# Local attention scores: 36 small products on eight array tiles for 18 products with padded queries

## The chip, the cores and the metric

The kernel runs on one core of a Trainium2 chip. The metric is the device time of one execution in microseconds (us), as the median of several runs. TensorE multiplies (PE in the profile; PEld is its weight loads), VectorE (DVE), ScalarE (ACT) and GpSimd (POOL) do the elementwise work, SyncE (SP) issues transfers. A product's *weights* are the operand that is loaded into the array, its *moving* operand streams through it. The array can be used in parts: a *tile* is a range of its rows and columns, given by the partitions that the operands and the result lie on.

## The reference

Attention over 8 batches and 8 heads with 576 positions of 64 channels, followed by a mixture of 8 experts that sends each token to one expert. The first four heads are local: a query sees the 32 positions that end at its own. The other four see every 32nd position.

```python
scores = scale * np.matmul(q, k.transpose(0, 1, 3, 2))
rel = pos[:, None] - pos[None, :]
mask_local = (rel >= 0) & (rel < stride)
mask_strided = (rel >= 0) & (pos[None, :] % stride == pos[:, None] % stride)
masks = np.stack([mask_local if h < H // 2 else mask_strided for h in range(H)], axis=0)
scores = np.where(masks[None, :, :, :], scores, -1000000000.0)
...
attn = attn / (np.sum(attn, axis=-1, keepdims=True) + 1e-09)
return np.matmul(attn, v).astype(np.float32)
...
for e in range(E):
    mask = e_idx == e
    h = np.maximum(x[mask] @ w1[e], 0.0)
    out[mask] = gate_w[mask, None] * (h @ w2[e])
```

## The kernel before

The attention is cut into 32 units that alternate: a local one (class `Local`, one head of two batches) and a strided one (class `Strided`, two heads of one batch). A unit passes through a pipeline of four steps. In round `n` of the loop over units TensorE does the scores of unit `n`, turns the exponentials of unit `n-2` (`turn`), writes the masks of unit `n+1` into PSUM (`masks`), and multiplies the values of unit `n-3` (`values`). This order on TensorE is written out by hand; the loads on SyncE keep the order of the program; the order on VectorE and ScalarE is set by a scheduler that works from estimated times. A few `warm` products on zeros fill the first rounds. After every four pairs of units a block of routing work (`lg`, `lt`, `en`) is spread over the next rounds. Then come the experts (`ffn`): weights and tokens are gathered, each split in two parts, and multiplied in three products each.

In a local unit a position's queries are cut into 18 blocks of 32. Block `i` of batch `bb` needs two neighbouring key blocks, 64 positions. The tile `qk` has the channels of batch 0 on partitions 0 to 63 and those of batch 1 on 64 to 127; its first 18 blocks are queries, the other 19 keys. So that one product does both batches over all 128 partitions, `prep` copies the queries into `qd`, which is zero elsewhere: batch 0's queries to rows 0 to 63, columns 0 to 31, batch 1's to rows 64 to 127, columns 32 to 63 (VectorE copies one half at L335, ScalarE the other at L333; there are two buffers `qd`, filled with zeros once at L296). The product then has 128 rows, 64 columns of weights and 64 moving columns. Its result lies on 64 partitions, so the 18 products of a unit take turns on two column tiles (`jj`). The nine groups `g` have their scores side by side in PSUM, four in one bank and five in another (`s`), on top of the masks. VectorE takes the maximum (`mx`) and subtracts it (`ex`), ScalarE exponentiates. `turn` transposes, ScalarE copies to `et`, and `values` multiplies with `vv`.

Of the kernel before, what the change touches and what calls it, by code (L numbers as in the profile page):

```python
# [20 lines left out]
P = 128  # L21
# [60 lines left out]
def _place(g, jj):  # L82

    return 16 + jj if g == 8 else 4 * (g // 2) + g % 2 + 2 * jj


def _block(i, bb):

    return (i + 2 * bb) % 18


def _constants():
    cf = np.zeros((P, C_N), np.float32)
    cf[:, C_ID:C_ID + P] = np.eye(P)
    cf[:, C_RE8:C_RE8 + E] = E - np.arange(E)
    cf[:, C_H:C_H + TH] = np.arange(P)[:, None] + P * np.arange(TH)
    cf[:, C_SIO:C_SIO + NBP * LA] = np.arange(NBP * LA)
    cf[:, C_P] = np.arange(P)
    cf[:, C_F:C_F + 4] = P * np.arange(4)
    for i, r0 in enumerate(ROWS):  # L100
        for t in range(4):
            cf[r0 + 18 * t:r0 + 18 * t + 18, C_T + 4 * i + t] = 1
    cb = np.zeros((P, M_N), np.float32)
    cb[:, M_ID:M_ID + P] = np.eye(P)
    qi = np.arange(32)[:, None]
    kk = np.arange(64)[None, :]
    for g in range(9):
        for jj in range(2):
            for bb in range(2):
                ok = (kk > qi) & (kk <= qi + STRIDE)  # L110
                if _block(_place(g, jj), bb) == 0:
                    ok = ok & (kk >= 32)
                r0 = 64 * jj + 32 * bb
                cb[r0:r0 + 32, M_L + 64 * g:M_L + 64 * g + 64] = np.where(ok, 0, BIG)
    a = np.arange(18)
    causal = np.where(a[None, :] <= a[:, None], 0, BIG)
    for j in range(2):
        for h in range(2):
            r0 = 64 * j + 18 * h
            cb[r0:r0 + 18, M_S:M_S + 288] = np.tile(causal, (1, 16))  # L120
    cb[:, M_TRI:M_TRI + P] = -(np.arange(P)[:, None] >= np.arange(P)[None, :]).astype(np.float32)
    cb[:, M_ONE:M_ONE + P] = 1
    tok = P * np.arange(36)[None, :] + np.arange(P)[:, None]
    return cf, cb.astype(ml_dtypes.bfloat16), tok.astype(np.float32)


def _layout(q, k, v, moe_modality_id, moe_w_gate, moe_modality_bias, moe_w1, moe_w2):
# [12 lines left out]
    for bb in range(2):  # L140
        for i in range(18):
            blk = _block(i, bb)
            qkl[:, :, bb, :, i] = qt[:, :, bb, :, blk]
            qkl[:, :, bb, :, 19 + i] = kt[:, :, bb, :, blk]
            w = win[:, :, i % 2, :, 2 * (i // 2) + bb] if i < 16 else win[:, :, i - 16, :, 16 + bb]
            w[:, :, 32:, :D] = vr[:, :, bb, blk]
            if blk:
                qkl[:, :, bb, :, 18 + i] = kt[:, :, bb, :, blk - 1]
                w[:, :, :32, :D] = vr[:, :, bb, blk - 1]
# [17 lines left out]
    mod = mod.reshape(36, P).transpose(1, 0)  # L167
    mb = np.broadcast_to(np.asarray(moe_modality_bias).reshape(1, 2 * E), (P, 2 * E))
    cf, cb, tok = _constants()
    rt = np.concatenate([wg.reshape(P, 128), np.ascontiguousarray(mod).view(np.float32), tok, mb], axis=1)  # L170
    nul = np.zeros((1, 2 + DM), np.int32)
# [20 lines left out]
def attention_moe(ctx: ExitStack, tc: tile.TileContext, a, out):  # L192
    nc = tc.nc
# [6 lines left out]
    def pa(name):  # L200
        return ps.tile([P, 512], F32, tag="a", name=name)
# [35 lines left out]
    pin = tc.keep_in_program_order  # L237
# [31 lines left out]
    def behind_units(ins, of=None):  # L269
        of = spots if of is None else of  # L270
        if of:
            tc.add_manual_dep(ins.ins, of[-1].ins.name, behind, reason="units first")
# [4 lines left out]
    def mark(ins):  # L277
        pace.append(ins)
# [10 lines left out]
    def zeros(n, shape, name):  # L289
        return [lp.tile(shape, F32, bufs=1, name=f"{name}{i}") for i in range(n)]  # L290

    qds = zeros(2, [P, 18, 2, 32], "qd")
    ets = zeros(1, [P, 18, 2, 32], "et")
    qzs = zeros(2, [P, 32, 2, 18], "qz")
    for t in qds + ets:
        nc.vector.memset(t[:], 0.0)  # L296
    for t in qzs:
        nc.gpsimd.memset(t[:], 0.0)
# [6 lines left out]
    class Local:  # L305
# [19 lines left out]
                self.vv.rearrange("p i c -> p (i c)")[:, c], a["vl"][self.bp, self.h, :, c]))  # L325

        def prep(self):
            self.qd = qd = qds[self.n % 2]
            for bb in range(2):
                r = slice(64 * bb, 64 * bb + 64)  # L330
                dst, src = qd[r, :, bb, :], self.qk[r, 0:18, :]
                if bb:
                    pin(nc.scalar.copy(dst, src))  # L333
                else:
                    ins = nc.vector.tensor_copy(dst, src)  # L335
                    pin(ins)
                    behind_units(ins)

        def masks(self):
            self.ss = []  # L340
# [3 lines left out]
                self.ss.append((g0, gn, s.rearrange("p (g c) -> p g c", g=gn)))  # L344

        def scores(self):
            n, qk, qd = self.n, self.qk, self.qd
            mx = lp.tile([P, 9], F32, tag="mx", name=f"mx{n}")
            self.ex = ex = lp.tile([P, 11, 64], F32, tag="ex", name=f"ex{n}")
            for g0, gn, s in self.ss:  # L350
                for g in range(gn):
                    for jj in range(2):
                        i = _place(g0 + g, jj)
                        self.scored = nc.tensor.matmul(  # L354
                            s[64 * jj:64 * jj + 64, g, :],
                            qd[:, i, :, :].rearrange("p b q -> p (b q)"),
                            qk[:, 18 + i:20 + i, :].rearrange("p b q -> p (b q)"),
                            start=False, stop=True, skip_group_check=True,
                        )
                m = mx[:, g0:g0 + gn]  # L360
                ins = nc.vector.tensor_reduce(m, s, AX.X, ALU.max)
                if g0:
                    behind_units(ins)
                nc.vector.tensor_tensor(ex[:, g0:g0 + gn, :], s, m.unsqueeze(2).to_broadcast([P, gn, 64]), ALU.subtract)
                nc.scalar.activation(ex[:, g0:g0 + 4, :], ex[:, g0:g0 + 4, :], AF.Exp, scale=0.125)
            nc.scalar.activation(ex[:, 9:11, :], ex[:, 8:9, :].to_broadcast([P, 2, 64]), AF.Exp, scale=0.125)
# [16 lines left out]
        def values(self):  # L383
            n, et, vv, xt, h = self.n, self.et, self.vv, self.xt, self.h
            for bb in range(2):
                gn = 5 - bb
                o = pa(f"o{n}{bb}")[:, :(D + 1) * gn].rearrange("p (g c) -> p g c", g=gn)
                for k in range(4):
                    for jj in range(2):
                        u = 4 * k + 2 * jj + bb  # L390
                        self.valued = nc.tensor.matmul(  # L391
                            o[64 * jj:64 * jj + 64, k, :], et[:, u, :, :].rearrange("p g q -> p (g q)"), vv[:, u, :],
                            start=True, stop=True, skip_group_check=True,
                        )
                if bb == 0:
                    for b2 in range(2):
                        nc.tensor.matmul(
                            o[64 * b2:64 * b2 + 64, 4, :], et[:, 16 + b2, :, :].rearrange("p g q -> p (g q)"),
                            vv[:, 16 + b2, :], start=True, stop=True, skip_group_check=True,
                        )  # L400
                rs = lp.tile([P, 5], F32, tag="rs", name=f"rs{n}{bb}")
                nc.vector.tensor_scalar(rs[:, :gn], o[:, :, D], 1e-9, None, ALU.add)
                nc.vector.reciprocal(rs[:, :gn], rs[:, :gn])
                mark(nc.vector.tensor_tensor(
                    xt[:, 5 * bb:5 * bb + gn, D * h:D * h + D], o[:, :, 0:D],
                    rs[:, :gn].unsqueeze(2).to_broadcast([P, gn, D]), ALU.mult,
                ))
# [759 lines left out]
    for what in ORDER.split():  # L1167
        i = int(what[1])
# [15 lines left out]
    for n in range(nu + 3):  # L1184
# [13 lines left out]
        if 1 <= n <= nu:  # L1198
            ins = units[n - 1].load_values(0)
# [8 lines left out]
        if 1 <= n <= nu:  # L1208
            ins = units[n - 1].load_values(1)
# [65 lines left out]
    li, _, inc, wall = tables[len(PHASES) - 1]  # L1275
# [38 lines left out]
```

## Time and profile before

| | us |
|---|---|
| Median of three runs (lowest, highest) | 584.99 (580.6, 586.03) |
| The profiled execution | 581.83 |
| Its span, first to last instruction | 580.0 |
| TensorE busy, modelled | 564.3 |
| VectorE, ScalarE, GpSimd busy | 381.7, 325.0, 197.2 |

Busy times are sums over the span. Matmuls overlap in the array, and their ends are modelled, so TensorE's busy time alone doesn't say how dense its work is; the chain of waits and the counts of records do. In the chain, "issue" is time in which an engine waited for nothing that the profile shows. A product of two float32 operands is two records in the trace, each with a weight load of its own.

### The profile page before, as it was taken

The page shows a single profiled execution, that of the slowest core. Times are in us where ns is not written, and L with a number is a line of the kernel's source. Part 1 is how long each engine was busy: PE and PEld are TensorE (multiplying, and loading weights), DVE is VectorE, ACT ScalarE, POOL GpSimd, SP SyncE. Part 2 cuts the span into 40 slices and gives each one's busy share as a digit, 9 for nine tenths or more (in the row PEclk, how much of TensorE's full clock was granted, in tenths as well). Part 3 has the DMA queues.
Part 4 walks back from the last instruction along what each step waited for, and adds up shares of the span by engine and source line. Part 5 has one row for each costly group of instructions (what it writes and reads, how often), then busy time and mean ns, then how long its engine had stood idle before and what let it go on. Part 6 is the DMA issues. An engine that isn't in the chain of part 4 may idle for free.

```text
span 580.0 us, 13584 instructions
## 1 busy us (share of the span) xinstructions
PE 564.3 (97%) x5383; PEld 495.1 (85%) x5385; DVE 381.7 (66%) x909; ACT 325.0 (56%) x646; POOL 197.2 (34%) x198
## 2 busy tenths in 40 slices
PE   9999999998999999999999999999999999999995
PEld 5878888877788899989999998989898998998884
DVE  7886977967867874676674757666475666655410
ACT  5789898897744544554454544545363555545312
POOL 3011120125464315444344334554434445320102
PEclk9999999999999999999999999999999999999999
DMA  8988898978985308566543266142414156772102
GB/s 299 332 287 298 287 326 292 327 229 296 313 296 196 118 12 308 187 199 223 154 164 74 61 211 216 47 88 73 90 33 99 52 200 174 262 162 72 56 0 76
DMA packets 62699, 104.28 MB, mean 180 GB/s; under 512 B 36451, under 2 KB 36963, under 8 KB 58532
## 3 DMA queue, kind: packets, MB, share of 16 engines
q0 software_dynamic: 15456, 57.47, 28.6%
q1 hardware_dynamic: 45636, 43.29, 25.5%
q10 hardware_dynamic: 1536, 2.58, 1.4%
q8 instruction: 44, 0.72, 0.5%
q14 instruction: 27, 0.22, 0.1%
HBM read 94.09 MB, written 19.18 MB: 195 GB/s over the span
## 4 chain that ended last, share of the span: by engine, by line
PE 82%; issue 10%; ACT 3%; DVE 2%; POOL 1%; POOLq 0%; ACTq 0%
PE h L1022 31%; PE o L1037 30%; PE s L354 3%; PE ss L449 3%; PE o L391 2%; PE ot L499 2%; PE lg L597 2%; PE xl L224 2%; PE t L224 2%; PE xs L224 1%; PE warm L212 1%; PE ts L224 1%; POOL out L1044 1%; ACT xc L507 1%; PE en L695 1%
## 5 line engine op out<-in xcount | busy, mean ns | idle before, releaser
L1059 DVE TENSOR_TENSOR wl<-raw,wh 128x512 fp32r<-128x512 f32 x176 | 115.2, 692 | 66.8 <-ACT wh L1058 56.7
L1058 ACT CAST wh<-raw 128x512 fp32r<-128x512 f32 x176 | 100.5, 619 | 99.4 <-PE o L1037 81.5
L1022 PE MATMUL h<-xh,wl 128*128 128x384 f32 x352 | 118.7, 337 | 0.0
L1022 PE MATMUL h<-xl,wh 128*128 128x384 f32 x352 | 118.2, 336 | 0.0
L1022 PE MATMUL h<-xh,wh 128*128 128x384 f32 x352 | 117.4, 337 | 0.0
L1037 PE MATMUL o<-wl,hh 128*128 128x512 f32 x264 | 104.1, 394 | 0.0
L1037 PE MATMUL o<-wh,hl 128*128 128x512 f32 x264 | 104.0, 395 | 0.0
L1037 PE MATMUL o<-wh,hh 128*128 128x512 f32 x264 | 103.2, 391 | 0.0
L1025 ACT ACTIVATE hh<-h 128x384 fp32r<-128x384 f32 x88 | 43.2, 491 | 82.4 <-PE h L1022 71.0
L1027 DVE SCALAR_TENSOR_TENSOR hl<-h,hh 128x384 fp32r<-128x384 f32 x88 | 48.9, 555 | 56.5 <-ACT hh L1025 55.1
L921 POOL DMA_INDIRECT raw<-in_w,wi x44 | 51.8, 1177 | 61.3 <-ACT hh L1025 50.8
L1022 PEld LDWEIGHTS h<-xh,wh 128*128 128x128 f32 x352 | 66.2, 188 | 4.2 <-PE xs L224 0.4
L1022 PEld LDWEIGHTS h<-xl,wh 128*128 128x128 f32 x352 | 66.1, 188 | 2.9
L1022 PEld LDWEIGHTS h<-xh,wl 128*128 128x128 f32 x352 | 66.0, 188 | 0.4 <-DVE wl L1059 0.4
L889 POOL DMA_INDIRECT fx<-xd,le x33 | 37.2, 1129 | 76.8 <-ACT wh L1058 42.2
L1037 PEld LDWEIGHTS o<-wh,hl 128*128 128x128 f32 x264 | 49.5, 188 | 10.5
L1037 PEld LDWEIGHTS o<-wl,hh 128*128 128x128 f32 x264 | 49.5, 188 | 8.6
L1037 PEld LDWEIGHTS o<-wh,hh 128*128 128x128 f32 x264 | 49.6, 188 | 8.2
L906 POOL DMA_INDIRECT le<-ld,li x33 | 35.5, 1076 | 41.9 <-DVE li L828 17.6
L1044 POOL DMA_INDIRECT out<-y,le x33 | 34.6, 1049 | 41.3 <-ACT y L1043 37.0
L589 POOL DMA_DIRECT2D xd<-xt x18 | 10.0, 558 | 64.9 <-ACT xc L507 28.2
L983 DVE COPY work<-fx 128x1536 uint16<-128x1536 uint16 x16 | 27.2, 1743 | 0.0
(215 smaller groups left out, 872.6 us busy)
## 6 DMA issues: line engine op xcount, KB each, us to landing
vv<-in_vl SPq DMA_DIRECT2D x32, 292.5 KB
qks<-in_qks SPq DMA_DIRECT2D x32, 288.0 KB
qk<-in_qkl SPq DMA_DIRECT2D x16, 304.0 KB
qk<-in_qkl SPq DMA_DIRECT2D x16, 288.0 KB
xd<-xt POOLq DMA_DIRECT2D x18, 256.0 KB
vsp<-in_vs SPq DMA_DIRECT2D x16, 256.0 KB
xd<-xt SPq DMA_DIRECT2D x9, 256.0 KB
xd<-xt ACTq DMA_DIRECT2D x2, 1024.0 KB
```

Source lines behind the costliest of these rows:

```text
L224: return nc.tensor.transpose(dst, src, ident)
L889: ins = in_turn(nc.gpsimd.indirect_dma_start(xt[:, h, :], None, xd[0:xrows, :], IOA(ap=le[:, h, 0:1], axis=0), **bounds))
L906: in_turn(nc.gpsimd.indirect_dma_start(le[:, h, :], None, ld[0:1 + last, :], IOA(ap=li[:, s, h:h + 1], axis=0)))
L921: ins = nc.gpsimd.indirect_dma_start(raws[j].rearrange("p f c -> p (f c)"), None, a["w"], IOA(ap=wi[:, s, j:j + 1], axis=0), bounds_check= ...
L983: pin(nc.vector.tensor_copy(rows[:, :, w, :], halves(xt)[:, :, :, w]))
L1022: nc.tensor.matmul(hp, w[:, a1], x[:, c, 0:size], start=(k == 0), stop=(k == 11))
L1025: steps.append(nc.scalar.activation(hh[:, 0:size], hp, AF.Relu))
L1027: nc.vector.scalar_tensor_tensor(hl[:, 0:size], hp, 0.0, hh[:, 0:size].bitcast(F32), ALU.max, ALU.subtract)
L1037: nc.tensor.matmul(os[h], hx[:, m], w[:, 512:1024], start=(f == 0 and i == 0), stop=(f == 7 and i == 2))
L1044: outs.add(in_turn(nc.gpsimd.indirect_dma_start(out, IOA(ap=le[:, i, 0:1], axis=0), y[:], None, bounds_check=NT - 1, oob_is_err=False), True))
L1058: nc.scalar.copy(wh[:, c], raw[:, c])
L1059: nc.vector.tensor_tensor(wl[:, c], raw[:, c], wh[:, c].bitcast(F32), ALU.subtract)
```

## The change

`prep` is empty, and `qd` with its zeros is gone. `scores` makes one product for each batch, block and group: 64 rows (the batch's partitions), 32 columns of weights (the block's queries, straight from `qk`) and 64 moving columns. There are 36 per unit. The result goes to 32 partitions; `_side` exchanges the two batches' partitions in the groups 4 to 8, so that a group of the first bank and one of the second together use all eight tiles of 64 rows by 32 columns. The groups run in the order 0, 4, 1, 5, 2, 6, 3, 7, 8, the maxima and subtractions stand behind all of them, and the masks and the index into `et` follow the exchange.

```diff
+def _side(g, bb):
+
+    return bb ^ (g >= 4)
...
-                r0 = 64 * jj + 32 * bb
+                r0 = 64 * jj + 32 * _side(g, bb)
...
-    qds = zeros(2, [P, 18, 2, 32], "qd")
...
         def prep(self):
-            self.qd = qd = qds[self.n % 2]
-            for bb in range(2):
-                r = slice(64 * bb, 64 * bb + 64)
-                dst, src = qd[r, :, bb, :], self.qk[r, 0:18, :]
-                if bb:
-                    pin(nc.scalar.copy(dst, src))
-                else:
-                    ins = nc.vector.tensor_copy(dst, src)
-                    pin(ins)
-                    behind_units(ins)
+            pass
...
-            for g0, gn, s in self.ss:
-                for g in range(gn):
-                    for jj in range(2):
-                        i = _place(g0 + g, jj)
+            for g in (0, 4, 1, 5, 2, 6, 3, 7, 8):
+                g0, _, s = self.ss[g >= 4]
+                for jj in range(2):
+                    for bb in range(2):
+                        i, r = _spot(g, jj, bb), slice(64 * bb, 64 * bb + 64)
+                        c0 = 64 * jj + 32 * _side(g, bb)
                         self.scored = nc.tensor.matmul(
-                            s[64 * jj:64 * jj + 64, g, :],
-                            qd[:, i, :, :].rearrange("p b q -> p (b q)"),
-                            qk[:, 18 + i:20 + i, :].rearrange("p b q -> p (b q)"),
+                            s[c0:c0 + 32, g - g0, :], qk[r, i, :], qk[r, 18 + i:20 + i, :].rearrange("p b q -> p (b q)"),
                             start=False, stop=True, skip_group_check=True,
                         )
+            for g0, gn, s in self.ss:
                 m = mx[:, g0:g0 + gn]
                 ins = nc.vector.tensor_reduce(m, s, AX.X, ALU.max)
...
-                            o[64 * jj:64 * jj + 64, k, :], et[:, u, :, :].rearrange("p g q -> p (g q)"), vv[:, u, :],
+                            o[64 * jj:64 * jj + 64, k, :],
+                            et[:, 4 * k + 2 * jj + _side(2 * k, bb), :, :].rearrange("p g q -> p (g q)"), vv[:, u, :],
```

`_spot(g, jj, bb)` returns `_place(g, jj)`.

On TensorE, round 4 (the third local unit) reads as follows before; the numbers behind the names are buffers, `x8` counts products:

```order
L354 MATMUL s_367<-qk_198,qd_101 64x64 x8
L354 MATMUL s_369<-qk_198,qd_101 64x64 x10
L224 MATMUL t_432<-cf_sb,ex_260 128x128 x4
L224 MATMUL t_437<-cf_sb,ex_260 128x128
L442 LDWEIGHTS cb_sb
L442 MATMUL ss_444<-cb_sb 128x288
L499 MATMUL ot_446<-eb_361,vsp_113 64x72 x8
L499 MATMUL ot_456<-eb_361,vsp_113 64x72 x8
```

The same place after:

```order
L356 MATMUL s_393<-qk_208 32x64 x4
L356 MATMUL s_395<-qk_208 32x64 x4
L356 MATMUL s_393<-qk_208 32x64 x4
L356 MATMUL s_395<-qk_208 32x64 x4
L356 MATMUL s_393<-qk_208 32x64 x4
L356 MATMUL s_395<-qk_208 32x64 x4
L356 MATMUL s_393<-qk_208 32x64 x4
L356 MATMUL s_395<-qk_208 32x64 x8
L234 MATMUL t_476<-cf_sb,ex_270 128x128 x4
L234 MATMUL t_481<-cf_sb,ex_270 128x128
L444 LDWEIGHTS cb_sb
L444 MATMUL ss_488<-cb_sb 128x288
```

The 18 products became 36, which go to the two banks by turns; what stands behind them is as it was, ten lines further down in the file.

On VectorE, behind the copy `qz` of a strided unit, before:

```order
L438 COPY qz_105<-qks_729 64x32x18
L361 TENSOR_REDUCE mx_901<-s_858 128x4
L468 RECIPROCAL sms_841<-sms_841 128x16
L364 TENSOR_TENSOR ex_902<-s_858,mx_901 128x256
L470 TENSOR_TENSOR enp_111<-exs_838,sms_841 128x288
L361 TENSOR_REDUCE mx_901<-s_860 128x5
L364 TENSOR_TENSOR ex_902<-s_860,mx_901 128x320
L335 COPY qd_101<-qk_802 64x18x32
L461 TENSOR_REDUCE mxs_1013<-ss_941 128x16
```

The corresponding place after:

```order
L440 COPY qz_103<-qks_787 64x32x18
L470 RECIPROCAL sms_915<-sms_915 128x16
L362 TENSOR_REDUCE mx_975<-s_932 128x4
L472 TENSOR_TENSOR enp_107<-exs_912,sms_915 128x288
L362 TENSOR_REDUCE mx_975<-s_934 128x5
L365 TENSOR_TENSOR ex_976<-s_932,mx_975 128x256
L365 TENSOR_TENSOR ex_976<-s_934,mx_975 128x320
L463 TENSOR_REDUCE mxs_1103<-ss_1033 128x16
```

The copy to `qd` is gone, and the second maximum moved ahead of the first subtraction.

## Rows read from the trace of the kernel before

**Rows 1.** Page, part 1: busy us (share) xinstructions, by engine.

```profile
PE 564.3 (97%) x5383; PEld 495.1 (85%) x5385; DVE 381.7 (66%) x909; ACT 325.0 (56%) x646; POOL 197.2 (34%) x198
```

**Rows 2.** Table by stretches: us, busy by engine, granted clock, DMA share, GB/s.

```profile
6.40:18.50 12.10, 11.99 (x301) 9.70 (x303) 10.24 (x30) 8.55 (x19) 0.00 (x0) 1.00 1.01 360
18.50:34.00 15.50, 14.19 (x397) 12.67 (x395) 13.32 (x41) 13.73 (x31) 2.65 (x6) 1.00 0.86 279
34.00:135.00 101.00, 97.83 (x2324) 83.21 (x2322) 81.95 (x319) 88.36 (x204) 18.13 (x28) 1.00 0.89 295
135.00:580.00 445.00, 435.04 (x2355) 387.56 (x2352) 272.39 (x517) 212.22 (x392) 171.78 (x155) 1.00 0.46 145
```

**Rows 3.** The same table for the local scores (L354) alone: PE, PEld.

```profile
0.00:18.50 18.50, 3.76 (x108) 3.40 (x108) 1.00 0.91 312
18.50:34.00 15.50, 2.66 (x72) 2.40 (x72) 1.00 0.86 279
34.00:135.00 101.00, 14.17 (x396) 12.51 (x396) 1.00 0.89 295
```

**Rows 4.** Chain of waits, 38 to 58 us: start us, us, what, records.

```profile
39.14 1.11 issue
...
48.31 1.20 PE s L354 x36
...
51.47 1.86 PE lg L597 x32
...
53.56 1.23 PE ss L449 x64
```

**Rows 5.** Chain of waits, 17 to 34 us.

```profile
18.60 0.59 ACT et L378
...
21.90 0.67 ACT qd L333
...
29.50 0.67 ACT qd L333
...
33.35 0.34 DVE xt L404
```

**Rows 6.** Groups of instructions by line: count, busy us, mean ns, idle before.

```profile
L333 ACT COPY qd<-qk 64x576 f32<-64x576 f32 x16 | 10.7, 668 | 2.7 <-DMA qk<-in_qkl 2.3
...
L335 DVE COPY qd<-qk 64x576 f32<-64x576 f32 x16 | 7.1, 445 | 0.2 <-DMA qk<-in_qkl 0.2
...
L364 DVE TENSOR_TENSOR ex<-s,mx 128x256 f32<-128x256 f32 x16 | 6.5, 406 | 0.0
...
L296 DVE MEMSET qd<- 128x1152 f32 x2 | 2.0, 1018 | 0.4 <-issue 0.4
```

**Rows 7.** Waits of TensorE's weight loads to 135 us: total us, times, longest.

```profile
PEld o L391 <- ACT xt L514: 0.9, 2, 0.5
```

**Rows 8.** Chain of waits, 0 to 150 us.

```profile
1.19 4.94 PE warm L212 x13
...
62.95 0.67 ACT qd L333
...
97.72 0.67 ACT qd L333
```

**Rows 9.** Chain of waits, 107 to 127 us.

```profile
109.22 1.00 PE en L695 x18
...
114.44 0.88 issue
...
125.52 0.36 issue
```

**Rows 10.** Table by stretches for `lg` (L597) alone, its first 0.03 us.

```profile
51.40:51.43 0.03, 0.03 (x4) 0.03 (x4) 1.00 0.65 230
```

**Rows 11.** TensorE's instruction queue: packets, MB, share; whole span (page), then 0 to 135 us.

```profile
q8 instruction: 44, 0.72, 0.5%
...
q8 instruction: 23, 0.38, 1.1%
```

More of the change, by code (lines that the diff above doesn't have):

```diff
@@ L84, in _place, with _spot @@
     return 16 + jj if g == 8 else 4 * (g // 2) + g % 2 + 2 * jj
+def _spot(g, jj, bb):
+    return _place(g, jj)
+def _side(g, bb):
+    return bb ^ (g >= 4)
 def _block(i, bb):
@@ L110, in _constants @@
                 ok = (kk > qi) & (kk <= qi + STRIDE)
-                if _block(_place(g, jj), bb) == 0:
+                if _block(_spot(g, jj, bb), bb) == 0:
                     ok = ok & (kk >= 32)
-                r0 = 64 * jj + 32 * bb
+                r0 = 64 * jj + 32 * _side(g, bb)
                 cb[r0:r0 + 32, M_L + 64 * g:M_L + 64 * g + 64] = np.where(ok, 0, BIG)
@@ L290, in zeros @@
         return [lp.tile(shape, F32, bufs=1, name=f"{name}{i}") for i in range(n)]
-    qds = zeros(2, [P, 18, 2, 32], "qd")
     ets = zeros(1, [P, 18, 2, 32], "et")
     qzs = zeros(2, [P, 32, 2, 18], "qz")
-    for t in qds + ets:
+    for t in ets:
         nc.vector.memset(t[:], 0.0)
@@ L346, in scores @@
         def scores(self):
-            n, qk, qd = self.n, self.qk, self.qd
+            n, qk = self.n, self.qk
             mx = lp.tile([P, 9], F32, tag="mx", name=f"mx{n}")
             self.ex = ex = lp.tile([P, 11, 64], F32, tag="ex", name=f"ex{n}")
-            for g0, gn, s in self.ss:
-                for g in range(gn):
-                    for jj in range(2):
-                        i = _place(g0 + g, jj)
+            for g in (0, 4, 1, 5, 2, 6, 3, 7, 8):
[4 more added lines that the diff above has]
+                        c0 = 64 * jj + 32 * _side(g, bb)
                         self.scored = nc.tensor.matmul(
-                            s[64 * jj:64 * jj + 64, g, :],
-                            qd[:, i, :, :].rearrange("p b q -> p (b q)"),
-                            qk[:, 18 + i:20 + i, :].rearrange("p b q -> p (b q)"),
+                            s[c0:c0 + 32, g - g0, :], qk[r, i, :], qk[r, 18 + i:20 + i, :].rearrange("p b q -> p (b q)"),
                             start=False, stop=True, skip_group_check=True,
                         )
+            for g0, gn, s in self.ss:
                 m = mx[:, g0:g0 + gn]
@@ L397, in values @@
                         nc.tensor.matmul(
-                            o[64 * b2:64 * b2 + 64, 4, :], et[:, 16 + b2, :, :].rearrange("p g q -> p (g q)"),
+                            o[64 * b2:64 * b2 + 64, 4, :], et[:, 16 + _side(8, b2), :, :].rearrange("p g q -> p (g q)"),
                             vv[:, 16 + b2, :], start=True, stop=True, skip_group_check=True,
```

## The prediction

> **What bounds the kernel now.** I read the page first: TensorE is busy for 97% of the span [rows 1]. The profiled execution took 581.83 us, its span 580.0, so 1.83 lie around it; the median of the three runs shown, 584.99, is 3.16 above that execution. I take differences from the profiled execution and subtract them from the median.
>
> The second view is the table by stretches [rows 2]. The local scores (L354) run only up to 135 us; the remaining 445 us are the experts' products, which the change doesn't touch. The granted clock is 1.00 in each stretch shown, so every price below is one at 2.4 GHz. Of the 16 local units three have their scores before 18.5 us, two up to 34 us and eleven between 34 and 135 us (36 records each) [rows 3]. The stretches have different limits. From 6.4 to 18.5 us the 16 DMA engines are full (share 1.01, 360 GB/s). From 34 to 135 us TensorE is busy for 97.8 of 101 us, VectorE and ScalarE for 82 and 88.
>
> The third view is the chain of waits. From 38 to 58 us it is one product after another on TensorE, with a single gap, and a local unit's scores stand in it with 1.20 us [rows 4]. So here a microsecond less on TensorE is a microsecond less in all, as long as the others keep up. From 18.6 to 33.7 us the same view runs through ScalarE and VectorE instead: the copies to `et`, to `xc`, and twice the copy to `qd` with 0.67 us [rows 5].
>
> **What the change removes.** Per local unit it removes the two copies that build `qd`, 0.67 us on ScalarE and 0.45 on VectorE, 16 of each, and at the start two fills of 1.0 us [rows 6]. In the stretch bound by ScalarE both `qd` copies are on the chain: 2 x 0.67 = **1.3 us** come off; the next that is late there is TensorE, which was busy for 14.19 of 15.5 us. Between 34 and 135 us the copies lie beside TensorE's work and I cost them at nothing. Twice the loads of `o` waited for ScalarE's copy to `xt`, 0.9 us in all [rows 7], and the chain has a `qd` copy ahead of such an `o` at 62.95 and at 97.72 us [rows 8]; so I leave out 0.9 us at most. The fills end before the first scores, behind which TensorE has its 4.94 us of `warm` [rows 8]: nothing.
>
> **What it does to the scores.** Before, a unit is 18 products with 64 columns of weights on two column tiles; after, 36 products with 32 columns of weights and half the rows, on eight tiles, and as many moving columns (64) in each. Each product is two records in the trace (36 and now 72). The price hangs on how many tiles run at once.
> One tile: `en` (L695) puts nine products of 64 moving columns into one place; 18 records take 1.00 us [rows 9], 55.6 ns for a record alone on its tile. Two tiles: the scores now, 18 records on each tile, 18 x 55.6 = 1.00 us, and 0.20 to fill and leave. Four tiles: `lg` (L597), eight records per tile of 256 columns, 8 x 4 x 55.6 = 1.78 us, and the chain shows 1.86 [rows 4]. Its records also start together: four products and four weight loads in the first 0.03 us [rows 10]. So the time was each tile's own records one after another plus 0.08 to 0.20, whatever the other tiles did, with one, two and four tiles. After the change the groups 4 to 8 give the busiest tile five products, ten records: 10 x 55.6 = 0.56, plus 0.18 = **0.74 us**, against 1.20. That saves 0.46 per unit.
> Eight tiles, and tiles that share columns but not rows, are not in this trace, so I bound the cost. Below: 72 records at the spacing in which `lg` starts (four in 0.03 us) are 0.54 us, so the tile's own time with the small lead, 0.64, is the floor. Above: the densest long stream is the strided scores, 64 records in 1.23 us, 19.2 ns each [rows 4]; 72 of these are 1.38 us, 0.18 more than now. I take 0.74, since `ss` also runs on two tiles only and loads 36 columns of weights for 18 moving ones, so that its pace is its tiles' and not the stream's.
> In the stretch that TensorE bounds: 11 x 0.46 = **5.1 us**. In the first 18.5 us three units could give 1.4; the DMA engines are full there, `warm` products stand between the units, and I take **0.5**.
>
> **What it adds.** TensorE's program grows by 16 x 36 x 2 = 1152 instructions. Its instructions come by a queue of their own: 44 packets, 0.72 MB in all, for 10,768 records, a packet of 16 KB per 245 of them [rows 1, 11]; 4.7 packets more. Up to 135 us there were 23 [rows 11], and three halts of TensorE inside a run of products with no waiter named: 1.11, 0.88 and 0.36 us [rows 4, 9]. 2.35/23 = 0.10 us per packet, so **0.5 us** more, if the halts are these packets' and come as often.
> On VectorE the order moves: both maxima now stand ahead of both subtractions, since both score tiles end together. A unit's scores end 0.46 us earlier, and its exponentials are needed two units later, so I cost the move at nothing; without that cover one subtraction, 0.41 us a unit [rows 6], would be late. The moved columns of `et` change an index only.
>
> **A rule against it.** Each pair of row halves writes the same PSUM bank in the same round (groups 0 and 4 have one bank each, with both halves in it). No row shows this, since every product before spans all row groups. The Trainium skill, TensorEngine Tiling (Array Packing), section Restrictions and Gotchas, says that different row tiles cannot access the same PSUM bank simultaneously. By that rule the first rival below would hold; its price is worked out from rows there.
>
> **Rivals.** (1) *The halves take turns*: four tiles at once, as in `lg`, and no more. Then 72/4 = 18 records follow each other per column group, as now: 1.20 us, no gain on TensorE. ScalarE's 1.3 us stay, and the 0.5 of the packets: 584.99 - 1.3 + 0.5 = **584.2**. For it: nothing in the trace runs more than four at once. Against it: with one, two and four tiles each tile kept its own time.
> (2) *The stream can't be fed, slower*: a unit takes 144 instructions in 0.74 us, 195 per us, where it took 72 in 1.20, 60 per us, and `ss` 104 per us. TensorE halts for 0.9 to 1.1 us when the next packet is late, as at 39.14 us, inside the scores themselves [rows 4]. If each of the eleven units met one halt of 1.0 us: 584.99 - 6.9 + 11.0 = **589.1**. It decides from seven more halts on. Against it: 20 of 23 packets came without such a halt, in a stretch where DMA moved 295 GB/s.
> (3) *The stream sets the pace*: if `ss` is as dense as records can follow each other, the unit takes the upper bound, 1.38 us, 11 x 0.18 = 2.0 more: 584.99 + 2.0 - 1.3 + 0.5 = **586.2**. Against it: the start of `lg`, four in 0.03 us [rows 10].
> The Trainium skill, TensorE: Matmul & The Clock Gate, section Wait — 56ns, not 53.3ns?, has such a floor: starts never come closer than about 25 ns. By that figure an estimate is 72 x 25 = 1.80 us a unit and 589.8 in all; `ss` with 19.2 ns a record lies under it already, so the trace does not agree.
> (4) *Another takes over*: with 5 us less in 101, the DMA engines (share 0.89 there) or VectorE are late instead, or the handover to the experts gives part back. Half the gain stays: **581.8**.
> (5) *More comes off*: 0.64 us a unit in 14 units (7.8), 1.3 and 0.9 on ScalarE: **575.0**.
>
> **How the numbers follow.** 5.1 + 1.3 + 0.5 - 0.5 = 6.4 us; 584.99 - 6.4 = **578.6**. Forecast 0.60, rival (1) 0.13, (2) 0.07, (3) 0.03, (4) 0.10, (5) 0.07. The forecast's own range is 576 to 581.5 (0.64 to 0.80 us a unit, 0 to 1.4 at the start, 0 to 1 of halts). The range goes on to rival (1) above and (5) below, with a little for the runs, which lay between 580.6 and 586.03: 574 to 586; outside are (2) and (3). About 1% (5.8 us) is what a measurement of this kernel tells from no change; 579.1 is the border. Of the forecast a little over half lies below it: 0.60 x 0.58 + 0.07 = 0.42 faster; slower is (2) with a little of the rest, 0.09; 0.49 within.
>
> **What would show it.** In the profile after: 72 score records per unit in about 0.74 us of the chain, over 1.15 if the halves take turns; eight products starting within some 60 ns; no `qd`; the chain between 18 and 34 us on TensorE again; halts without a waiter inside the scores, three to five in all, not ten; the experts' first products some 6 us earlier and the rest shifted with them. I am wrong if the score stage isn't shorter, or if it is and the experts start no earlier.

## The result, and the profile after

The changed kernel is slower: 589.96 us, median of four runs (588.73 to 593.4), against 582.86 of the kernel before, now also of four (580.6 to 586.03); the ratio is 1.014, 95% interval 1.0096 to 1.0184. The forecast was 578.6, the range ended at 586. The profiled execution took 589.28 us with a span of 587.5, 7.5 more than before.

The page first: busy time of TensorE (matmuls, weight loads), the granted clock in 40 slices, and the queue of instructions (packets, MB, share of the DMA engines).

```profile
PE 565.4 (96%) x5961; PEld 494.0 (84%) x5961; DVE 373.7 (64%) x891; ACT 313.2 (53%) x630; POOL 194.2 (33%) x198
...
PEclk9999979999999999999999999999999999999999
...
q8 instruction: 49, 0.80, 0.6%
```

There are 578 more matmul records than in [rows 1] (16 x 36 = 576 by the code; a few are missing there), five more instruction packets than in [rows 11], and one slice at a lower clock. The table by stretches answers to [rows 2], with the third one cut where the clock changes.

```profile
6.40:18.50 12.10, 10.54 (x374) 7.99 (x377) 8.15 (x22) 6.26 (x16) 0.00 (x0) 1.00 0.97 336
18.50:34.00 15.50, 13.20 (x476) 11.37 (x469) 12.19 (x40) 11.67 (x28) 1.52 (x5) 1.00 0.84 267
34.00:72.00 38.00, 36.04 (x1003) 30.70 (x1004) 28.37 (x104) 29.66 (x72) 4.64 (x8) 1.00 0.88 288
72.00:82.00 10.00, 7.97 (x188) 6.74 (x183) 6.03 (x20) 4.63 (x11) 3.01 (x5) 0.66 0.83 281
82.00:135.00 53.00, 50.28 (x1371) 41.82 (x1370) 38.89 (x161) 40.15 (x97) 7.84 (x13) 1.00 0.87 281
```

In every stretch shown TensorE, VectorE, ScalarE and the DMA engines are less busy than before (34 to 135 us: TensorE 94.3 us after, 97.8 before): nobody has taken over as the bound. The chain of waits (start, us, what) shows a unit's scores, and further on the worst place:

```profile
51.56 0.90 PE s L356 x61
...
71.82 0.42 PE ss L451 x17
72.23 2.03 issue
74.27 1.63 PE ss L451 x46
75.90 1.02 PE ts L234 x4
76.92 0.48 PE s L343 x2
77.40 1.07 PE o L392 x16
78.47 0.21 PE o L399 x4
78.68 0.87 PE o L392 x16
79.55 1.05 PE xs L234 x4
80.59 0.92 PE s L356 x61
```

The scores take 0.90 us where they took 1.20 [rows 4]. But TensorE stands still for 2.03 us inside the strided scores, with no releaser named, and afterwards everything up to 80.6 us takes nearly twice its time: the granted clock of this stretch is 0.66, a mix of the levels 2.4 and 1.2 GHz. At full clock these pieces take 3.5 us (46 x 19.2 ns of `ss`, 0.57, 0.24, 0.62, 0.12, 0.47 and 0.59, as elsewhere in the chain); they took 6.3, so the clock cost 2.8.

TensorE's waits up to 125 us, by line and releaser (us, times, longest):

```profile
PE s L356 <- issue: 4.3, 4, 1.6
PE ss L451 <- issue: 3.6, 5, 2.0
PE o L392 <- issue: 1.6, 1, 1.6
...
PE ts L234 <- issue: 0.3, 1, 0.3
```

That is 9.8 us of halts without a releaser. The same view of the kernel before has 3.1, of which 2.0 on its chain and 1.1 at 23.6 us, where ScalarE was the bound. To see what these halts are, I counted TensorE's records from the start up to the inside of a halt (window, length, then matmuls and weight loads, x). First the changed kernel:

```profile
0.00:11.00 11.00, 9.73 (x222) 5.26 (x222) 4.79 (x13) 4.21 (x8) 4.64 (x10) 1.00 0.83 280
...
0.00:25.30 25.30, 22.10 (x599) 15.37 (x599) 15.40 (x45) 13.49 (x31) 4.64 (x10) 1.00 0.90 302
...
0.00:39.90 39.90, 34.31 (x974) 25.67 (x974) 26.41 (x77) 23.80 (x56) 7.29 (x16) 1.00 0.87 289
0.00:72.40 72.40, 65.22 (x1856) 52.13 (x1856) 50.43 (x169) 49.46 (x117) 10.80 (x22) 1.00 0.87 285
0.00:104.20 104.20, 94.82 (x2611) 76.98 (x2611) 70.43 (x237) 70.79 (x168) 15.96 (x31) 0.97 0.87 285
0.00:108.40 108.40, 98.44 (x2737) 80.05 (x2738) 74.12 (x255) 74.28 (x177) 16.50 (x32) 0.97 0.87 282
```

and the two large halts of the kernel before, at 39.14 and 114.44 us [rows 4, 9]:

```profile
0.00:39.40 39.40, 36.52 (x846) 28.62 (x848) 32.16 (x90) 29.57 (x65) 7.29 (x16) 1.00 0.90 305
0.00:114.70 114.70, 110.09 (x2606) 91.75 (x2609) 93.87 (x324) 94.84 (x215) 18.84 (x37) 1.00 0.92 306
```

The sums are 444, 1198, 1948, 3712, 5222 and 5475 records, and 1694 and 5215 before. The distances are 754, 750, 1764, 1510 and 253, and 3521 before: 3, 3, 7, 6, 1 and 14 times some 252. A packet of instructions holds 245 records on average over the program (10,768 in 44). So TensorE halts where it goes over from one packet to the next. All eleven of the changed kernel's halts up to 125 us stand at such places; of those of the kernel before in [rows 4, 9] only the small one at 125.52 us doesn't.

The trace also has the times at which the packets moved. Around the largest halt (72.23 to 74.27 us) the DMA view of 71.5 to 72.8 us has one packet of the instruction queue, and that of 72.8 to 74.3 none:

```profile
q8 instruction: 1, 0.02, 5.3%
```

5.3% of 16 engines' 1.3 us is 1.1 us; by its record the packet moved from 71.66 to 72.77 us, and TensorE went on 1.50 us later. All eleven halts end in this way, 1.20 to 1.55 us behind the landing of an instruction packet, and the three of the kernel before 1.28 to 1.41. In all sixteen kernels of this document 123 of 126 halts up to 125 us end 1.0 to 1.7 us behind such a landing (the others are one in e5 and two in e8). So the cause of the halts doesn't rest on the distances alone.

### The profile page after: what moved, and what is told of

It reads as the page before. It is cut to its first block, busy times and chain, and to the rows that moved or that the text cites. A ratio compares the mean times of both kernels' runs of the same rounds, so it can differ in the third digit from the quotient of the medians.

```text
span 587.5 us, 14699 instructions
## 1 busy us (share of the span) xinstructions
PE 565.4 (96%) x5961; PEld 494.0 (84%) x5961; DVE 373.7 (64%) x891; ACT 313.2 (53%) x630; POOL 194.2 (33%) x198
## 4 chain that ended last, share of the span: by engine, by line
PE 85%; issue 11%; POOL 1%; ACT 1%; DVE 1%; POOLq 0%; ACTq 0%
PE h L1024 31%; PE o L1039 29%; PE ss L451 3%; PE o L392 3%; PE ot L501 3%; PE s L356 3%; PE t L234 2%; PE xs L234 2%; PE ts L234 2%; PE xl L234 2%; PE warm L222 1%; PE lg L599 1%; POOL out L1046 1%; PE en L697 1%; PE s L343 1%
## 5 line engine op out<-in xcount | busy, mean ns | idle before, releaser
L891 POOL DMA_INDIRECT fx<-xd,le x33 | 35.5, 1075 | 76.2 <-ACT wh L1060 23.7
```

The costliest lines, as they stand in the source:

```text
L891: ins = in_turn(nc.gpsimd.indirect_dma_start(xt[:, h, :], None, xd[0:xrows, :], IOA(ap=le[:, h, 0:1], axis=0), **bounds))
```

## The experiments

Theory A: TensorE's instructions come late, and the change, with twice the instructions in the scores, makes this worse. Rival B: the eight tiles or their density do it. Rival C: the lost copies, and the order that they leave on the other engines, do it. "Halts" are TensorE's waits without a releaser up to 125 us, in one profiled execution; "instructions" are those of the local and the strided scores of two neighbouring units, two for each matmul record.

| kernel | instructions | time over before (interval) | halts, us (times) |
|---|---|---|---|
| before | 200 | 1 | 3.1 (3) |
| changed | 272 | 1.0140 (1.0096, 1.0184) | 9.8 (11) |
| e1 | 272 | 1.0146 (1.0105, 1.0187) | 9.6 (10) |
| e2 | 200 | 0.9999 (0.9972, 1.0026) | 3.4 (4) |
| e3 | 200 | 0.9895 (0.9856, 0.9933) | 5.3 (7) |
| e4, fewer loads | 272 | 0.9962 (0.9936, 0.9989) | 4.1 (5) |
| e5, fewer loads | 200 | 0.9934 (0.9912, 0.9956) | 1.4 (3) |
| e6 | 256 | one execution | 11.2 (12) |
| e7 | 272 | 1.0112 (1.0042, 1.0183) | 11.1 (12) |
| e8 | 164 | 0.9988 (0.9954, 1.0022) | 4.7 (8) |
| e9 | 284 | 1.0212 (1.0164, 1.0260) | 7.3 (10) |
| e10 | 208 | 0.9946 (0.9910, 0.9981) | 12.9 (8) |
| e11 | 164 | 0.9918 (0.9877, 0.9958) | 3.1 (3) |
| e12 | 136 | 0.9724 (0.9670, 0.9778) | 0.5 (1) |
| e13 | 256 | one execution | 9.2 (12) |
| e14 | 272 | one execution | 18.7 (17) |

**e1: the instructions alone.** The kernel before with each product cut in two:

```diff
-self.scored = nc.tensor.matmul(
-    s[64 * jj:64 * jj + 64, g, :],
-    qd[:, i, :, :].rearrange("p b q -> p (b q)"),
...
+for bb in range(2):
+    c0 = 64 * jj + 32 * bb
+    self.scored = nc.tensor.matmul(
+        s[c0:c0 + 32, g, :], qd[:, i, bb, :],
...
```

> The kernel before, copies to qd and all, but each score product is cut into two of 32 columns of weights (128 rows, four column tiles): 36 products and 144 instructions a unit as in the changed kernel, no row halves, no eight tiles. Theory A, the supply of TensorE's instructions: 49 packets on the instruction queue, halts without a waiter rise from 2.4 us to 8 to 11 us up to 145 us, scores about 1.2 us a unit, time 590 to 594. Rival B, the eight tiles or their density (144 instructions in 0.9 us) make the halts: halts stay near 2.4 us and the time near 583. Rival C, the lost copies and the changed order on VectorE and ScalarE cost the time: 583, since both are as before.

588.85 us against 579.13. The chain's score piece, and the count inside three halts:

```profile
56.17 1.14 PE s L356 x72
```

```profile
0.00:12.50 12.50, 11.02 (x222) 5.98 (x222) 8.06 (x19) 5.64 (x10) 4.95 (x10) 1.00 0.81 268
...
0.00:43.30 43.30, 37.53 (x976) 28.36 (x977) 31.30 (x85) 27.88 (x61) 7.60 (x16) 0.96 0.82 265
...
0.00:112.70 112.70, 101.89 (x2742) 82.72 (x2742) 81.97 (x271) 84.37 (x190) 16.82 (x32) 0.97 0.85 273
```

With the copies, VectorE's order and four column tiles kept, it loses as much as the whole change, and it halts after the same 444, 1953 and 5484 records (the changed kernel: 444, 1948, 5475). Theory A holds; B and C fall.

**e2: the copies alone.** The kernel before with `if self.n >= 2: return` ahead of the copies in `prep`.

> The kernel before with the copies to qd made for the first two units only; the other units' scores use those stale queries, so the output is not the reference's. Everything else is as before. Theory A: 1 to 2 us less (580.9 to 581.9), halts as before (2.4 us). Rival C, that without the copies the loads and the other engines fall into a worse order: slower, 586 to 590.

Nothing came off, 579.13 against 579.13. The chain from 22 to 31 us, in the stretch that ScalarE bounded before [rows 5]:

```profile
22.73 0.52 PE s L356 x17
23.25 1.18 issue
24.43 0.80 PE s L356 x19
...
28.30 0.59 PE ts L224 x4
28.89 1.73 issue
30.62 0.41 PE s L345 x2
```

TensorE is on the chain there as soon as ScalarE isn't, and two packets in a row are late, 2.9 us. C's slowdown isn't there either.

**e3: one record per product.** The changed kernel with the upper halves of the operands:

```diff
-n, qk = self.n, self.qk
+n, qk = self.n, self.qk.bitcast(BF16)[:, :, 1::2]
```

> The changed kernel, but each score product takes the upper 16 bits of its fp32 operands as bf16, so that it is one record and not two: 36 records and 72 instructions a unit, as many as in the kernel before, on the same eight tiles and twice as dense in products; the scores are less exact. Theory A: 44 packets, halts back to 2 to 4 us, scores 0.4 to 0.5 us a unit, time 573 to 577. Rival B (eight tiles or density): halts stay at 8 us or more, time 580 or more. Rival C: 583 or more.

574.19 us against 579.13, scores 0.38 us:

```profile
40.34 0.38 PE s L356 x31
```

With the instructions of before, the same tiles win 1%, the small end of the gain that A forecast; part of it is the shorter products. The halts fell to 5.3 us, not to 2 to 4.

**e4 and e5: fewer loads.** In both forms a load of `vl` or `qks` takes a ninth of its columns from the third unit on:

```diff
-c = slice(9 * part * (D + 1), 9 * (part + 1) * (D + 1))
+c = slice(9 * part * (D + 1), 9 * part * (D + 1) + (9 * (D + 1) if n < 2 else 64))
...
-self.qk[:, part, :], a["qks"][self.b, self.pr, :, S * part:S * part + S]
+w = S if n < 2 else 64
...
+self.qk[:, part, :w], a["qks"][self.b, self.pr, :, S * part:S * part + w]
```

> The changed kernel, but from the third unit on the loads of the local values and of the strided queries and keys move a ninth of their columns (the rest stays as the first two units left it, so the output is not the reference's): about 15 MB less of the 40 MB that the DMA engines move up to 145 us. Theory A1, the instruction packets come late because they stand behind data: halts fall from 10.6 us to under 4, no stretch at half clock, time 576 to 582. Theory A2, the number or density of instructions alone makes TensorE wait, whatever else the DMA engines do: halts 8 to 11 us, time 586 to 590.

> The kernel before with the loads cut as in e4 (from the third unit on a ninth of the columns of the local values and of the strided queries and keys; the output is not the reference's). Theory A1, in the changed kernel the instruction packets are late because they stand behind data: the kernel before, with few halts to lose, gains little from it, 0 to 4 us, and ends within 2 us of e4, whose form then costs nothing. Rival, fewer loads shorten any form of the kernel for reasons of their own: 8 to 12 us less than before, and e4 stays some 8 us slower than this.

Each against its own runs of the kernel before, the changed form goes from 1.0140 to 0.9962 (10 us), the other from 1 to 0.9934 (3.8 us). Table by stretches, e4:

```profile
34.00:72.00 38.00, 37.45 (x1118) 31.60 (x1115) 30.78 (x112) 31.59 (x76) 6.17 (x12) 1.00 0.61 176
72.00:145.00 73.00, 71.37 (x1933) 60.53 (x1928) 60.52 (x248) 61.70 (x149) 20.38 (x28) 1.00 0.68 208
```

The DMA share is 0.61 to 0.68 instead of 0.83 to 0.88, the instructions are as many, and six of the eight us that the change costs are gone: A1. One halt of 2.3 us stayed at 20.4 us, and with it a granted clock of 0.78 from 18.5 to 34 us, so the forecast "no stretch at half clock" missed.

**e6, e7: what sets the 0.90 us.** e6 leaves out group 8 (`for g in (0, 4, 1, 5, 2, 6, 3, 7)`), e7 takes `for g in range(9)`.

> The changed kernel without the products of the ninth group (their scores stay at the mask, so the output is not the reference's): 32 products, 64 records, eight on each of the eight tiles, 128 instructions a unit. If each tile's own records set the time, as the prediction had it, scores take 8 x 55.6 ns and 0.18, 0.62 us; if the stream of instructions has a pace of its own (0.90 us for 72 records, 12.5 ns each), 0.80. Time by theory A: 583 to 588, with fewer halts than the changed kernel's 10.6 us.

> The changed kernel with its groups in the order 0 to 8, so that four tiles run for the first four groups and the other four for the last five, instead of the eight in turn; instructions as many as in the changed kernel. If each tile's own records set the pace: 8 x 55.6 + 10 x 55.6 ns and 0.18, 1.0 to 1.2 us a unit; if the stream does, 0.90 again. Theory A by number of instructions: halts of 8 to 11 us, time 1.2 to 1.8% over before; if it was the density of the eight tiles that made the packets late: halts of 3 to 6 us, time 0.3 to 0.9% over before.

e6: 0.79 us, as a pace of 12.4 ns a record would have it; e7: 1.03 us, as the tiles' own records would. So neither. Their halts are alike: 11.2 us (12) in e6, whose one execution took 589.2 us, and 11.1 in e7, which runs four tiles at a time and has fewer instructions per microsecond in the scores than the changed kernel (144 in 1.03 us, not in 0.90). The halts don't need the eight tiles.

**e8, e11: the old form with upper halves.** e8 is the kernel before with `.bitcast(BF16)[..., 1::2]` on `qk` and `qd`; e11 adds e2's line.

> The kernel before, copies to qd and all, with the upper 16 bits of the score products' fp32 operands as bf16: 18 records and 36 instructions a unit on two column tiles; the scores are less exact. Theory A (the instructions' number sets the halts, the copies cost nothing): 42 packets, halts under 3 us, scores 0.55 to 0.7 us a unit, time 0.8 to 1.4% under before, within 2 us of e3, whose eight tiles then bring nothing of their own. Rival, the eight tiles and the missing copies are worth something once the packets come in time: e3 stays 4 us or more faster than this.

> The kernel of e8 with the copies to qd made for the first two units only (stale queries after, so the output is not the reference's). If the copies on ScalarE and VectorE are what took e8's gain: 0.9 to 1.4% under before, as e3. If it is the eight tiles that give e3 its time: within 0.4% of before, as e8.

e8 gains nothing although its scores take 0.41 us; without the copies (e11) it is 0.8% under before, with e3's 1.05% inside its interval. So the rival of e8 was right, by the copies: they cost nothing while TensorE bounds, and some 4 us once its work shrinks. An estimated 1.5 us of that is the clock's: against the kernel before beside it, the median granted clock is 0.0045 lower in e8 (0.9925 against 0.997) and 0.002 in e11 (0.994 against 0.996), and the 0.0025 between them is 1.5 of 580 us. The eight tiles have no gain of their own that these runs can tell. TensorE's waits in e8 up to 145 us show the copies' engines, VectorE foremost:

```profile
PE rk L665 <- DVE cum L646: 2.3, 2, 1.1
...
PE ts L224 <- DVE enp L471: 1.0, 1, 1.0
PE en L696 <- POOL hv L690: 1.0, 1, 1.0
PE en L696 <- DVE rs L404: 0.9, 1, 0.9
```

It also showed that fewer instructions than before don't make fewer halts: 4.7 us, of which all but 0.7 end behind the landing of a packet.

**e9, e10: number or rate.** e9 puts six wide products of zeros behind the scores; e10 takes the upper halves in the strided scores:

```diff
+for _ in range(3):
+    for g0, gn, s in self.ss:
+        self.scored = nc.tensor.matmul(
+            s.rearrange("p g c -> p (g c)"), idle[:, 0:P], idle[:, 0:64 * gn],
+            start=False, stop=True, skip_group_check=True)
```

```diff
-n, qz, s = self.n, self.qz, self.s
+n, s = self.n, self.s
+qz, kk = (t.bitcast(BF16) for t in (self.qz, self.qk))
+qz, kk = qz[:, :, :, 1::2], kk[:, :, 1::2]
...
-self.qk[:, 1, 18 * r:18 * r + 18],
+kk[:, 1, 18 * r:18 * r + 18],
```

> The changed kernel with six wide products of zeros behind each unit's scores (bf16, 12 instructions, added to the same banks, 0.72 us of TensorE's time by the two mask products' 0.24): more instructions, but fewer per microsecond from the scores to the strided values, about 85 instead of 102 (the kernel before: 70). Theory R, the halts follow the rate at which instructions are used up: halts 4 to 8 us, time 1.6 to 2.2% over before. Theory N, they follow their number: halts 10 to 14 us, time 2.4 to 3% over before.

> The changed kernel, its local scores as they are, with the strided scores' products on the upper 16 bits of their operands (bf16, 32 records instead of 64 a unit; these scores are less exact): a local and a strided unit have 208 instructions in their scores, 200 in the kernel before, 272 in the changed one. Theory N: the number is back, so halts 2 to 5 us, and the scores' 0.30 us and some 0.6 us of the strided ones come off: 1.3 to 2% under before. Theory R: the stretch from the local scores to the strided values is as dense as in the changed kernel, so halts stay at 8 us or more and the time within 1% of before.

e9's time fits the rate. Its halts are 7.3 us up to 125 us, as the rate has it, but its attention lasts longer, and up to 148 us the chain has 10.3, as the number has it. e10's time and halts fit the rate; its ten executions spread from 574.12 to 582.37 us, and the profiled one is the longest, with halts of 3.8 and 2.6 us. The spread goes with the granted clock: 0.993 to 0.999 in the three shortest, 0.985 and 0.987 in the two longest. Inconclusive: neither number nor rate alone tells how many packets come late.

**e12: both upper halves.** e3 and e10 together.

> The changed kernel with both the local and the strided score products on the upper 16 bits of their operands (less exact scores): 136 instructions in the scores of a local and a strided unit. It is the version that should beat both kernels. By the supply of instructions (N): halts under 4 us, 46 packets or fewer, and 0.6 us per strided unit below e3: 1.8 to 2.6% under before. If VectorE or ScalarE is the bound by then: no faster than e3, 0.9 to 1.3% under before.

563.98 us against 579.45, 2.8% under before: better than N forecast, and faster than both kernels, at the price of less exact scores. Its products are also shorter, so not all of the gain is the instructions'. Its largest waits up to 125 us, and the one halt:

```profile
PE ot L503 <- ACT et L379: 1.7, 2, 1.2
PE o L392 <- DMA vv<-in_vl: 1.7, 3, 0.7
...
PE s L356 <- issue: 0.5, 1, 0.5
```

**e13, e14: the 0.90 us again.** e13 is e6 with `c0 = 64 * jj` and a bank for each row half, e14 has 32 moving columns instead of 64.

> The kernel of e6 (32 products, 64 records a unit), but all products go to two column tiles, each with both row halves, so to four tiles instead of eight; each half writes a bank of its own, over the masks, so the output is not the reference's. If the stream of instructions has a pace of its own (12.4 ns a record): scores 0.79 us as in e6. If each tile's own 16 records set the time: 16 x 55.6 ns, 0.9 to 1.07 us. If the two halves of a column tile take turns: 32 records one after another, 1.57 to 1.78 us.

> The changed kernel with 32 moving columns instead of 64 in each local score product (only the first half of each window is scored, so the output is not the reference's); products, records, instructions and tiles as in the changed kernel. If the stream has a pace of its own: scores 0.90 us again. If the records on a tile, or on a column tile in turn, set the time: they get shorter with their columns, 0.45 to 0.6 us.

A unit's scores in the chain of e13 and of e14:

```profile
51.21 1.03 PE s L358 x64
```

```profile
53.37 0.75 PE s L356 x50
```

e13: each tile's own records, 16 x 55.6 ns and 0.14; the two row halves of a column tile run at once. e14: 0.75, between the stream's 0.90 and the tiles' 0.45 to 0.6. So four tiles keep their own pace, and eight don't: part of the price hangs on the moved columns and part doesn't. What sets it stays open. (e13 took 589.54 us and e14 596.62, one execution each, against 582.28.)

e14 bears on the halts too: with the changed kernel's number of instructions in shorter scores it has 18.7 us of them, against 9.8. That speaks for the rate. But e3 has 72 instructions in 0.38 us, as dense as e14's 144 in 0.75, and 5.3 us, and e14 ran once.

## Why the prediction was wrong

**The step that failed** is "What it adds": 2.35/23 = 0.10 us of halts per packet, times 4.7 packets, 0.5 us. Five packets did come, but the price isn't one per added packet. Every packet of the attention can be late, and more of them were: on the chain, from 2.0 us of halts at packet boundaries to 9.9 (the eleven, by their pieces), 7.9 us more. One of these, of 2.03 us, was followed by the lower clock: 2.8 more, a term that the prediction didn't have; e7, with 11.1 us of halts, loses 1.1% at a granted clock of 0.993 to 0.998, so the halts alone are enough for most of the loss. With the scores' gain, -3.3 + 7.9 + 2.8 = 7.4; the span grew by 7.5. That it closes so well is partly luck: 4.3 of the halts lie before 34.4 us, where the sum counts no gain of the five units' scores, and what changed behind 125 us isn't in it. (Of the three halts that the 2.35 was made of, the one of 0.36 is no packet's, and one of 1.13 at 23.6 us was overlooked; 3.1 in 22 packets would have made it 0.7 us, so this slip isn't what failed.)

**Rival (2)** gave 589.1, and 589.96 came. So near a number is luck: it stood on a median before of 584.99, now 582.86, and as a change it was 4.1 us, where 7.1 came. It had the right mechanism, but placed it wrongly: it put the halts into the scores, for their density, while only 4 of 11 stand there, and e1 and e7 have as many at a lower density. The argument against it, that 20 of 23 packets had come without a halt while the DMA engines moved 295 GB/s, was the mistake: packets that came in time say nothing of how little they had to spare. Counted at 252 records each, 18 of the changed kernel's 23 packets between 18 and 125 us landed less than 1.65 us ahead of their first record, as the late ones do; before, 3 of 20 did. And e4 shows that the traffic makes the difference.

**The scores** were sized too short: 0.90 instead of 0.74 us, so 11 x 0.30 = 3.3 instead of 5.1. The tile's own 55.6 ns held with four tiles (e13) and not with eight.

**ScalarE's 1.3 us** didn't come (e2). "The next that is late there is TensorE" was right, but TensorE there meets late packets, and these took what the copies gave back. That the copies cost nothing between 34 and 135 us was right for the kernel as it was; e8 and e11 show that it stops being so once TensorE has less to do.

**Rival (1)** fell: 0.90 is under 1.15, and in e13 both halves run at once. The Trainium skill, TensorEngine Tiling (Array Packing), section Restrictions and Gotchas, says that different row tiles cannot access the same PSUM bank simultaneously. By that, e7, where each group's four products share a bank with two on either half, would have only two tiles at work, 36 x 55.6 ns = 2.0 us; it took 1.03. Here the halves write different partitions of the bank, and for that case the traces don't agree with the rule. **Rivals (3), (4) and (5)** fell too: a unit isn't slower, no engine is busier than before in the table by stretches, and the time rose. (The estimate of 589.8 beside rival (3) is a slip: with that rival's terms, 6.6 us more on TensorE make 590.8. Nothing hangs on it.)

**Not settled**: what decides which packets come late. More instructions (e1), and more data beside them (e4, e5), make it worse; e8 has fewer instructions than before and no fewer halts. When a packet was asked for, the trace doesn't show; when it began to move, it does. Between 18 and 125 us in the changed kernel that was 1.0 to 4.3 us, 2.1 on average, after TensorE had gone over to the packet ahead of it (252 records counted for each); in e4, with less data beside it, 1.4 on average. The one that ended the halt of 2.03 us began to move after 3.3.

## What to carry to other kernels

Where small products fill TensorE, count its instructions as a load of their own: here each 250 or so must arrive between data packets, and halving the work of a product while doubling the records lost 1.4%, where the same scores with half the changed kernel's records, and shorter ones (e12), came out 2.8% under before. Count records up to each unexplained halt, and look when the instruction packets land: equal distances, and a landing just ahead of each halt's end, point to them. And a late packet costs more than its own wait when the clock falls behind it, so a small gain per unit isn't safe where it makes the instruction stream denser.

## What was not expected of the hardware

- Halts at instruction packets come after the same number of records in different kernels (444, 1948 and 5475 in the changed one; 444, 1953 and 5484 in e1), and grew from 3.1 to 9.8 us with the change. 0.80 MB of instructions come during the execution, by a queue that shares the DMA engines with the data, and a halt ends 1.0 to 1.7 us behind the landing of a packet (123 of 126 halts).
- The granted clock was 0.66 from 72 to 82 us after a halt of 2.03 us, and 0.78 from 18.5 to 34 us in e4 after one of 2.3; after halts of 1.56 and 1.57 us in the changed kernel it stayed at 1.00.
- Two row halves of the array work at the same time, also into one PSUM bank on different partitions (e7: 1.03 us for 72 records on four tiles at a time).
